# Threshold attention and a tanh MoE: shared score tiles, a sign mask ahead of the transposes, and one hand-written schedule

## The chip, the cores and the metric

The kernel runs on one core of one Trainium2 chip. The metric is the device time of one execution in microseconds (us), the median of several runs. The engines that matter here are TensorE (PE, matmuls and transposes), VectorE (DVE), ScalarE (ACT), GpSimd (POOL) and SyncE (SP), which issues the DMAs.

## What is computed

Eight batches of eight heads; each head has 576 tokens and 64 dimensions. Weights more than `tau` (0.02) below their row's greatest score are dropped. The result, 4608 tokens by 512, goes through two matmuls with `h - tanh(h)` between them.

```python
scores = scale * np.matmul(q, k.transpose(0, 1, 3, 2))      # per head 576 x 576
thresh = np.max(scores, axis=-1, keepdims=True) - tau
scores = np.where(scores >= thresh, scores, -1000000000.0)
scores = scores - np.max(scores, axis=-1, keepdims=True)
attn = np.exp(scores)
attn = attn / (np.sum(attn, axis=-1, keepdims=True) + 1e-09)
out = np.matmul(attn, v)                                    # 576 x 64
x = out of all heads side by side                           # 4608 x 512
h = x @ w_in                                                # 512 x 2048
g = h - np.tanh(h)
y = g @ w_out                                               # 2048 x 512
```

## The kernel before

**Weights.** Lines 70 to 76 load `w_in` and `w_out` whole (4 MB each) on SP's queue and cast them to bf16 on POOL. They stand first in the program, so the first `q` load (line 97) is behind them on the queue and in its buffers.

**Attention** (lines 88 to 250) loops over 8 batches and 4 pairs of heads; a pair is 32 times the same work. For each head `q` and `k` are loaded, scaled by 256 and split into a high and a low fp16 half by ACT (line 112) and DVE (line 115). PE turns the five 128-row chunks (line 122), DVE copies the result (line 130). `kT_sw` is `kT` with its two 64-partition halves swapped, made by two DMAs (lines 135 and 138), so that two matmul sets per score tile give all products of high and low halves.

Then five query tiles (`qt`) of 128 rows, the last of 64, for each of the two heads: 320 score tiles in all. One tile is four score matmuls into `psS` (lines 177 and 182), `exp` on ACT (line 188), the row maximum on DVE (line 193), the threshold (line 197), compare, multiply and row sum on DVE (line 201), the reciprocal (line 207), five transposes of the weights on PE into `psPT` (line 213), their copy by ACT or DVE (lines 226 and 222), five matmuls with `v` (line 232), the scaling on ACT (line 238). Once per pair of heads and query tile the 128 columns are turned (line 244) and copied into `xT` (line 248).

**MoE** (lines 265 to 297) loops over nine blocks of 512 tokens: sixteen groups of four matmuls (line 271), each followed by `tanh` on ACT (line 278) and `th * -1 + psH` on DVE (line 279), and then four output tiles of sixteen matmuls each (line 287), copied by ACT (line 294) and stored.

**Order and buffers.** A scheduler orders the instructions and places the waits; each engine runs its own list in order. PSUM in attention: two `psS`, one `psT`, three shared by `psPT`, `psO` and `psOT`. In MoE: four `psH` and four `psY`.

## Time and profile before

| what | us |
|---|---|
| median of 3 runs | 1140.91 (1138.82 to 1142.63) |
| span of the profiled execution, first to last instruction | 1138.1 |
| weights loaded and cast, no matmul yet | 0 to 36 |
| attention | 36 to 885 |
| MoE alone | 885 to 1138 |

The page gives the span of the profiled execution and no time around it; the runs lie 0.7 to 4.5 us above that span, their median 2.8 above.

How to read the views. In the page's slices each digit is a tenth. In the busy table each row is a stretch of the span; after its length come PE, weight loads, DVE, ACT and POOL, each as busy us and, in brackets, its instructions; then the mean granted clock of TensorE (1.00 is its upper level of 2.4 GHz, 0.50 its lower of 1.2 GHz) and the DMA engines' share. A group of instructions shows its line, engine, operation, tiles and shapes, its count after the x, then busy us and the mean ns of one, and the idle time ahead of it with what ended it. In the timeline x5 means five instructions in a row, and the length is from the first one's start to the last one's end.

### The profile page before, as it was taken

What the parts mean: (1) busy time and instruction counts of PE and PEld (TensorE: products, weight loads), DVE (VectorE), ACT (ScalarE), POOL (GpSimd) and SP (SyncE); (2) the same over time, 40 slices, a digit from 0 to 9 for tenths busy, and PEclk for the clock granted to TensorE, in tenths of its full rate; (3) what the DMA queues carried; (4) which work ended last, traced back from release to release, by engine and by line L of the source; (5) the groups of instructions that cost most, each with busy time, mean ns of one, the idle gap of its engine ahead of it and who ended that gap; (6) DMA issues with size and microseconds to landing.
All of it is one profiled execution on the core that took longest, in us unless ns stands there. A gap on an engine that the chain in (4) does not pass through costs nothing.

```text
span 1138.1 us, 19514 instructions
## 1 busy us (share of the span) xinstructions
PE 858.6 (75%) x6408; PEld 479.1 (42%) x6432; DVE 787.3 (69%) x2289; ACT 589.8 (52%) x1141; POOL 121.7 (11%) x650
## 2 busy tenths in 40 slices
PE   0576777677777777677777777776777899999998
PEld 0244444444444444444444444444444444444443
DVE  0588887888888888888787788888887433333443
ACT  0456555555555655555555565556555444444443
POOL 4211111111111111111111111111110000000000
PEclk9978666766766877766676677778777899999999
DMA  7321112222222111112122222111110001111111
GB/s 295 73 48 43 43 43 48 48 53 49 48 50 46 42 43 42 44 42 47 44 51 49 49 50 51 43 43 43 42 43 6 19 37 47 38 37 37 44 41 37
DMA packets 134854, 56.85 MB, mean 50 GB/s; under 512 B 119392, under 2 KB 127584, under 8 KB 134240
## 3 DMA queue, kind: packets, MB, share of 16 engines
q1 hardware_dynamic: 134752, 55.61, 18.8%
q8 instruction: 50, 0.82, 0.3%
q14 instruction: 52, 0.43, 0.1%
HBM read 36.70 MB, written 9.44 MB: 41 GB/s over the span
## 4 chain that ended last, share of the span: by engine, by line
PE 52%; DVE 19%; ACT 18%; issue 6%; DMA 3%; POOL 1%; DVEq 0%; SPq 0%; ACTq 0%; POOLq 0%
PE psH L271 11%; PE psY L287 11%; ACT e L188 10%; DVE pr L201 6%; PE psPT L213 6%; PE psO L232 6%; PE psT L122 6%; PE psS L177 6%; DVE m L193 5%; ACT pT L226 4%; PE psS L182 4%; ACT o L238 3%; DVE pT L222 2%; PE psOT L244 2%; DMA w_out_f<-in_moe_w_out_dram 2%
## 5 line engine op out<-in xcount | busy, mean ns | idle before, releaser
L188 ACT ACTIVATE e<-psS,exp_bias 128x576 f32<-128x576 f32 (+1 forms) x320 | 234.1, 742 | 65.8 <-PE psS L182 48.2
L201 DVE SCALAR_TENSOR_TENSOR pr<-e,thr 128x576 bf16<-128x576 f32 (+1 forms) x320 | 255.2, 805 | 4.6 <-DVE thr L197 1.8
L193 DVE TENSOR_REDUCE m<-e 128x1 f32<-128x576 f32 (+1 forms) x320 | 235.0, 743 | 15.8 <-ACT e L188 15.3
L232 PE MATMUL psO<-vbf,pT 128*128 128x64 bf16 (+1 forms) x1600 | 123.7, 218 | 127.1 <-ACT pT L226 79.8
L238 ACT ACTIVATE o<-psO,recip 128x64 bf16<-128x64 f32 (+1 forms) x320 | 100.7, 315 | 221.4 <-PE psO L232 217.0
L177 PE MATMUL psS<-kT,qT 128*128 128x512 f16 (+3 forms) x640 | 165.9, 351 | 59.3 <-ACT e L188 40.4
L279 DVE SCALAR_TENSOR_TENSOR g_sb<-th,psH 128x512 bf16<-128x512 f32 x144 | 98.8, 688 | 137.5 <-ACT th L278 137.5
L182 PE MATMUL psS<-kT_sw,qT 128*128 128x512 f16 (+3 forms) x640 | 175.2, 348 | 0.0
L213 PE MATMUL psPT<-ident_bf,pr 128*128 128x128 bf16 (+1 forms) x1600 | 164.6, 246 | 1.7 <-DVE pr L201 1.1
L232 PEld LDWEIGHTS <-pT 128*128 128x128 bf16 (+1 forms) x1600 | 81.4, 115 | 184.5 <-ACT pT L226 115.0
L226 ACT COPY pT<-psPT 128x640 bf16<-128x640 bf16 x192 | 123.6, 644 | 36.9 <-PE psPT L213 33.8
L271 PE MATMUL psH<-xT,w_in_sb 128*128 128x512 bf16 x564 | 127.8, 383 | 2.8 <-DVE g_sb L279 1.5
L287 PE MATMUL psY<-w_out_sb,g_sb 128*128 128x512 bf16 x564 | 125.0, 379 | 0.6
L213 PEld LDWEIGHTS <-pr 128*128 128x128 bf16 (+1 forms) x1600 | 113.7, 114 | 22.2 <-DVE qhl L115 6.9
L177 PEld LDWEIGHTS <-qT 128*128 128x128 f16 (+1 forms) x640 | 64.1, 112 | 101.9 <-issue 80.2
L278 ACT ACTIVATE th<-psH 128x512 f32<-128x512 f32 x144 | 85.6, 597 | 39.6 <-PE psH L271 39.2
L209 POOL MEMSET pr<- 128x64 bf16 (+1 forms) x320 | 44.0, 150 | 438.7 <-PE psPT L213 267.5
L271 PEld LDWEIGHTS <-w_in_sb 128*128 128x128 bf16 x576 | 56.7, 99 | 70.2 <-issue 4.8
L222 DVE COPY pT<-psPT 128x640 bf16<-128x640 bf16 (+1 forms) x128 | 57.5, 449 | 40.9 <-PE psPT L213 38.9
L287 PEld LDWEIGHTS <-g_sb 128*128 128x128 bf16 x576 | 56.3, 98 | 68.0
L122 PE MATMUL psT<-ident_f,qhl 128*128 128x128 f16 (+1 forms) x320 | 50.2, 294 | 37.0 <-DVE qhl L115 37.0
L182 PEld LDWEIGHTS <-qT 128*128 128x128 f16 (+1 forms) x640 | 56.7, 118 | 50.7 <-issue 31.1
(33 smaller groups left out, 606.3 us busy)
## 6 DMA issues: line engine op xcount, KB each, us to landing
kT_sw<-kT SPq DMA_DIRECT2D x128, 72.0 KB, 2.0
out_dram<-yo SPq DMA_DIRECT2D x36, 256.0 KB, 2.0
qraw<-in_q_dram SPq DMA_DIRECT2D x64, 128.0 KB, 2.3
kraw<-in_k_dram SPq DMA_DIRECT2D x64, 128.0 KB, 2.2
vraw<-in_v_dram SPq DMA_DIRECT2D x64, 128.0 KB, 2.3
w_in_f<-in_moe_w_in_dram SPq DMA_DIRECT2D x1, 4096.0 KB, 12.6
w_out_f<-in_moe_w_out_dram SPq DMA_DIRECT2D x1, 4096.0 KB, 22.9
qraw<-in_q_dram SPq DMA_DIRECT2D x64, 16.0 KB, 2.2
```

The costliest lines, as they stand in the source:

```text
L122: nc.tensor.matmul(out=psT[:, c * P : c * P + cn], lhsT=hl[:cn, c, :, :].rearrange("p a d -> p (a d)"), rhs=ident_f16[:cn, :cn], is_transp ...
L177: nc.tensor.matmul(out=psS[:qn, kk0:kk1], lhsT=lhs, rhs=kT[:, kk0:kk1], start=True, stop=False,)
L182: nc.tensor.matmul(out=psS[:qn, kk0:kk1], lhsT=lhs, rhs=kT_sw[:, kk0:kk1], start=False, stop=True,)
L188: nc.scalar.activation(out=e0[:qn, :S], in_=psS[:qn, :S], func=ACT.Exp, scale=scale_eff, bias=exp_bias[:qn],)
L193: nc.vector.tensor_reduce(out=m0[:qn], in_=e0[:qn, :S], axis=AX.X, op=ALU.max,)
L201: nc.vector.scalar_tensor_tensor(out=pr[:qn, :S], in0=e0[:qn, :S], scalar=thr[:qn], in1=e0[:qn, :S], op0=ALU.is_ge, op1=ALU.mult, accum_ou ...
L213: nc.tensor.matmul(out=psPT[:, c * qn : (c + 1) * qn], lhsT=pr[:qn, c * P : (c + 1) * P], rhs=ident_bf[:qn, :qn], is_transpose=True, start ...
L226: nc.scalar.copy(out=pT[:, : KC * qn], in_=psPT[:, : KC * qn])
L232: nc.tensor.matmul(out=psO[:qn, :], lhsT=pT[:, c * qn : (c + 1) * qn], rhs=vb[:, c, :], start=(c == 0), stop=(c == KC - 1),)
L238: nc.scalar.activation(out=o2[:qn, hh * D : hh * D + D], in_=psO[:qn, :], func=ACT.Copy, scale=recip[:qn],)
L271: nc.tensor.matmul(out=psH, lhsT=w_in_sb[:, c, n * P : (n + 1) * P], rhs=xT[:, c, m0 : m0 + MB], start=(c == 0), stop=(c == DM_C - 1),)
L287: nc.tensor.matmul(out=psY, lhsT=g_sb[:, n, ms * P : (ms + 1) * P], rhs=w_out_sb[:, n, :], start=(n == 0), stop=(n == DF_C - 1),)
```

## The change

The new kernel computes the same by other tiles and in an order that is written out.

- **Tiles.** A pair of heads has nine score tiles (`TPP`) in place of ten: four of 128 queries for each head, and one (j = 4) whose upper 64 partitions are the first head's last 64 queries and whose lower 64 are the second's. That makes 288 tiles. `load`, `split`, `turn` work on a pair: one transposed `kT` and `qT` of 1152 columns each, nine transposes.
- **Mask.** `scores` ends in one DVE instruction that scales the scores from PSUM into `sc` and takes the row maximum; POOL makes `nb = tau - max`. `kink` is one ACT instruction, `Prelu` with a slope of 1e30 below zero: kept scores become `score - max + tau`, dropped ones hugely negative. `weights` turns this `z` on PE into `psZ`, and the `exp` is taken while ACT copies `psZ` out. The row sum comes from a column of ones behind `v` (65 columns in `attend`). `norm` divides for up to five tiles at once, `emit_x` turns and copies a whole pair into `xT`.
- **Split.** After the first pair, the high and low halves are made on POOL by three instructions, not by ACT and DVE.
- **MoE.** Once a batch of four pairs is done, the next batch's 36 rounds carry up to 32 steps of MoE. A step is either four matmuls of one hidden group with tanh and DVE (`h_step`) or four of the sixteen matmuls of an output tile of the block before (`y_step`). Seven of ten stages ride along (208 steps); the last three (80 steps) come at the end, with more PSUM buffers.
- **Weights of MoE** are loaded in sixteen pieces of 512 KB during the first batch, through two buffers, and cast on POOL.
- **PSUM.** Two double banks for scores and turned `q`, `k` (`ps_big`), and one bank each for `psZ` and `psX`, for `psO`, for `psH`, for `psY`.
- **Order.** `manual_schedule` keeps the order of the code on each engine. Round s holds: scores of tile s+3, `kink` of s+1, `weights` of s, a step of MoE, `attend` of s-1, and at fixed places `norm`, `emit_x`, `split`, `turn`, loads.

The lines that go are those of the kernel above from 53 to 297 and aren't repeated; of the new ones the core stands here.

```diff
+    ps_big = pool("ps_big", 2, space=PSUM)
+    ps_z = pool("ps_z", 1, space=PSUM)
+    ps_o = pool("ps_o", 1, space=PSUM)
+    ps_h = pool("ps_h", 1, space=PSUM)
+    ps_y = pool("ps_y", 1, space=PSUM)
+    ctx.enter_context(tc.manual_schedule())
...
+    def split(p, t, fast=False):
+        r = raws.pop((p, t))[:, 0:9, :]
+        hl = hl_pool.tile([P, TPP, 2, D], FP16, name=f"{t}hl", tag=t)
+        if fast:
+            nc.scalar.mul(out=hl[:, :, 0, :], in_=r, mul=QKSC)
+            nc.vector.scalar_tensor_tensor(
...
+            x = hl_pool.tile([P, TPP, D], F32, name="xs", tag="xs")
+            nc.gpsimd.tensor_scalar(
+                out=x, in0=r, scalar1=QKSC, scalar2=1.0, op0=ALU.mult, op1=ALU.mult
+            )
+            nc.gpsimd.tensor_copy(out=hl[:, :, 0, :], in_=x)
+            nc.gpsimd.tensor_tensor(
+                out=hl[:, :, 1, :], in0=x, in1=hl[:, :, 0, :], op=ALU.subtract
+            )
...
+    def turn(p, t):
+        hl = hls.pop((p, t))
+        ps = ps_big.tile([P, W], FP16, name=f"ps_{t}", tag="big")
+        for c in range(TPP):
+            nc.tensor.matmul(
+                out=ps[:, c * P : (c + 1) * P],
+                lhsT=hl[:, c, :, :].rearrange("p a d -> p (a d)"),
+                rhs=ident_f16, is_transpose=True, start=True, stop=True,
+            )
+        m = qk_pool.tile([P, W], FP16, name=f"{t}T", tag=t)
+        nc.vector.tensor_copy(out=m, in_=ps)
+        mats[p, t] = m
+        if t == "k":
+            sw = qk_pool.tile([P, W], FP16, name="kS", tag="ks")
+            nc.sync.dma_start(out=sw[0:D, :], in_=m[D:P, :])
+            nc.sync.dma_start(out=sw[D:P, :], in_=m[0:D, :])
...
+    def kind(j):
+        return "M" if j == 4 else "A" if j in (0, 2, 5, 7) else "B"
+    def scores(i):
+        p, j = divmod(i, TPP)
+        qT, kT, kS = mats[p, "q"], mats[p, "k"], mats[p, "ks"]
+        ps = ps_big.tile([P, 1024], F32, name="psS", tag="big")
+        main, rem, lo = slice(0, 512), slice(512, 576), 0
+        if kind(j) == "B":
+            main, rem, lo = slice(512, 1024), slice(448, 512), 448
+        if j == 4:
+            for n, kk in enumerate((kT, kS)):
+                for dst, srcs in ((main, MAIN), (rem, REM)):
+                    for hh in range(2):
...
+            hh = int(j > 4)
+            lhs = qT[:, j * P : (j + 1) * P]
+            for n, kk in enumerate((kT, kS)):
+                for dst, src in ((main, MAIN[hh]), (rem, REM[hh])):
+                    nc.tensor.matmul(
+                        out=ps[:, dst], lhsT=lhs, rhs=kk[:, src],
+                        start=(n == 0), stop=(n == 1),
+                    )
+        sc = sc_pool.tile([P, S], F32, name="sc")
+        mx = st_pool.tile([P, 1], F32, name="mx", tag="mx")
+        nc.vector.tensor_scalar(
+            out=sc, in0=ps[:, lo : lo + S], scalar1=SC, scalar2=None,
+            op0=ALU.mult, op1=ALU.max, accum_out=mx,
+        )
+        nb = st_pool.tile([P, 1], F32, name="nb", tag="nb")
+        nc.gpsimd.tensor_scalar(
+            out=nb, in0=mx, scalar1=-1.0, scalar2=tau, op0=ALU.mult, op1=ALU.add
+        )
+        scs[i] = sc, nb
...
+    def kink(i):
...
+        else:
+            zt = z_pool.tile([P, W], BF16, name="z")
+            zs[i] = zt
+            z = zt[:, 0:S]
+        nc.scalar.activation(
+            out=z, in_=sc, func=ACT.Prelu, bias=nb, scale=1.0, alpha=STEEP
+        )
...
+    def weights(i):
+        kd = kind(i % TPP)
+        ps = ps_z.tile([P, 5 * P], BF16, name="psZ", tag="z")
+        if kd == "B":
+            z, pt, off, n = zs.pop(i - 1), pts[i - 1], 512, 5
+        else:
+            z = zs[i] if kd == "A" else zs.pop(i)
+            pt = p_pool.tile([P, TPP * P], FP16, name="pT")
+            pts[i] = pt
+            off, n = 0, 4
+        for c in range(n):
...
+        nc.scalar.activation(
+            out=pt[:, off : off + n * P], in_=ps[:, 0 : n * P], func=ACT.Exp
+        )
...
+    def attend(i):
...
+        if j in (1, 6):
+            ops[p, int(j > 4)] = ps_o.tile([P, 5, D + 1], F32, name="psO", tag="o")
+        po = ops[p, int(j > 4)]
...
+        pt, hh = pts.pop(i - 1), int(j > 4)
+        for ab in range(2):
+            blocks = [(4 * ab + ab + c, c) for c in range(4)]
+            blocks.append((4, 4 + ab))
+            for n, (blk, c) in enumerate(blocks):
+                nc.tensor.matmul(
+                    out=po[:, (j - 1 - 5 * hh) + ab, :],
+                    lhsT=pt[:, blk * P : (blk + 1) * P], rhs=vb[:, hh, c, :],
+                    start=(n == 0), stop=(n == 4),
                 )
...
+    def norm(p, hh):
...
+        nc.vector.reciprocal(out=rc[:, 0:n], in_=po[:, 0:n, D])
+        nc.vector.tensor_tensor(
+            out=osb[p][:, 0:n, hh, :], in0=po[:, 0:n, 0:D],
+            in1=rc[:, 0:n].unsqueeze(2).to_broadcast([P, n, D]), op=ALU.mult,
+        )
...
+    def emit_x(p):
...
+        ps = ps_z.tile([P, S], BF16, name="psX", tag="z")
+        for t in range(4):
+            nc.tensor.matmul(
+                out=ps[:, t * P : (t + 1) * P],
...
+        nc.vector.tensor_copy(out=xT[:, p % HPAIR, b * S : (b + 1) * S], in_=ps)
...
+    def hidden(m, n, ps):
...
+        for c in range(DM_C):
+            nc.tensor.matmul(
+                out=ps, lhsT=w_in_sb[:, c, n * P : (n + 1) * P],
+                rhs=xT[:, c, m * MB : (m + 1) * MB],
+                start=(c == 0), stop=(c == DM_C - 1),
+            )
+        th = t_pool.tile([P, MB], F32, name="th")
+        nc.scalar.activation(out=th, in_=ps, func=ACT.Tanh)
+        nc.vector.scalar_tensor_tensor(
+            out=gs[m][:, n, :], in0=th, scalar=-1.0, in1=ps,
+            op0=ALU.mult, op1=ALU.add,
+        )
...
+    def project(m, ms, part, ps, last):
+        for n in range(4 * part, 4 * part + 4):
+            nc.tensor.matmul(
+                out=ps, lhsT=gs[m][:, n, ms * P : (ms + 1) * P],
+                rhs=w_out_sb[:, n, :], start=(n == 0), stop=(n == DF_C - 1),
+            )
+        if part == 3:
+            yo = y_pool.tile([P, d_model], F32, name="yo")
+            if last:
+                nc.scalar.copy(out=yo, in_=ps)
+            else:
+                nc.vector.tensor_copy(out=yo, in_=ps)
...
+    def layers(m, tail):
...
+        def h_step(n):
+            if tail and n % 3:
+                ps = ps_big.tile([P, MB], F32, name="psHt", tag="big")
+            else:
+                ps = ps_h.tile([P, MB], F32, name="psH", tag="h")
+            hidden(m, n, ps)
+        def y_step(ms, part):
+            if part == 0:
+                tag = ("y", "o", "z")[(4 * (m - 1) + ms) % 3] if tail else "y"
+                pl = {"y": ps_y, "o": ps_o, "z": ps_z}[tag]
+                cur["y"] = pl.tile([P, d_model], F32, name="psY", tag=tag)
+            project(m - 1, ms, part, cur["y"], tail and ms % 2)
...
+        for a in range(16):
+            if m < NMB:
+                steps.append(lambda a=a: h_step(a))
+            if m > 0:
+                steps.append(lambda a=a: y_step(a // 4, a % 4))
+        return steps
...
+    def w_load(piece):
...
+        nc.gpsimd.tensor_copy(out=flat[:, i * cols : (i + 1) * cols], in_=wt)
...
+    load(0)
+    load(1)
+    for t in ("k", "q"):
+        split(0, t, fast=True)
+        turn(0, t)
+    split_v(0)
...
+    for s in range(-AHEAD, NTILE + 2):
+        p, j = divmod(max(s, 0), TPP)
+        if 0 <= s < NTILE and j == 0 and p % HPAIR == 0 and p >= HPAIR:
+            assert not todo
+            todo = layers(stage, False)
+            share = len(todo) / (HPAIR * TPP)
+            done, stage = 0.0, stage + 1
+        if s + AHEAD < NTILE:
+            scores(s + AHEAD)
+        if 0 <= s + 1 < NTILE:
+            kink(s + 1)
+        if 0 <= s < NTILE:
+            weights(s)
+            if todo:
+                done += share
+                if j == TPP - 1 and p % HPAIR == HPAIR - 1:
+                    done = 1e9
+                while todo and done >= 1:
+                    todo.pop(0)()
+                    done -= 1
+        if 0 <= s - 1 < NTILE:
+            attend(s - 1)
+            pp, jj = divmod(s - 1, TPP)
+            if jj == 4:
+                norm(pp, 0)
+            if jj == 8:
+                norm(pp, 1)
+                emit_x(pp)
+        if 0 <= s < NTILE:
+            if j == 0 and p + 2 < NPAIR:
+                load(p + 2)
+            if p + 1 < NPAIR:
+                if j == 0:
+                    split(p + 1, "k")
+                if j == 1:
+                    split(p + 1, "q")
+                if j == 2:
+                    split_v(p + 1)
+                    turn(p + 1, "k")
+                if j == 4:
+                    turn(p + 1, "q")
+            if p < HPAIR and j >= 3:
+                piece = next(pieces, None)
+                if piece:
+                    w_load(piece)
+    while stage <= NMB:
+        for step in layers(stage, True):
+            step()
+        stage += 1
```

On ACT, in the midst of attention, there stood (names as above, the number is the buffer):

```order
L188 ACTIVATE e0_5824<-psS_5819,exp_bias_68 128x576
L226 COPY pT_5706<-psPT_5700 128x640
L188 ACTIVATE e0_5860<-psS_5855,exp_bias_68 128x576
L238 ACTIVATE o2_5650<-psO_5708,recip_5697 128x64
L188 ACTIVATE e0_5892<-psS_5887,exp_bias_68 128x576
L226 COPY pT_5742<-psPT_5736 128x640
L238 ACTIVATE o2_5718<-psO_5744,recip_5733 128x64
L188 ACTIVATE e0_5928<-psS_5923,exp_bias_68 64x576
L238 ACTIVATE o2_5718<-psO_5776,recip_5765 128x64
```

and now stands, in a batch with MoE steps:

```order
L240 ACTIVATE z_5168<-sc_5126,nb_5129 128x576
L266 ACTIVATE pT_5189<-psZ_5188 128x512
L240 ACTIVATE z_5257<-sc_5163,nb_5166 128x576
L266 ACTIVATE pT_5189<-psZ_5259 128x640
L351 ACTIVATE th_5271<-psH_5266 128x512
L240 ACTIVATE z_5257<-sc_5182,nb_5185 128x576
L266 ACTIVATE pT_5291<-psZ_5290 128x512
L240 ACTIVATE z_5341<-sc_5252,nb_5255 128x576
L266 ACTIVATE pT_5291<-psZ_5343 128x640
L351 ACTIVATE th_5355<-psH_5350 128x512
L240 ACTIVATE z_5368<-sc_5284,nb_5287 128x576
L266 ACTIVATE pT_5371<-psZ_5370 128x512
```

Each tile has one `Prelu` (L240) and one `exp` out of PSUM (L266); the `Prelu` of tile s+1 is ahead of the `exp` of tile s, and a tanh (L351) comes behind the `exp` in four rounds of nine. Copies, scalings and splits are gone from ACT, and the list holds a single table load, at its start, as before.

On DVE, where a query tile or a pair ends, there stood:

```order
L222 COPY pT_6398<-psPT_6392 128x320
L115 SCALAR_TENSOR_TENSOR khl_6469<-kraw_6465,khl_6469 128x5x64
L193 TENSOR_REDUCE m0_6498<-e0_6496 128x1
L248 COPY xT_70<-psOT_6407 128x64
L130 COPY kT_6478<-psT_6472 128x576
L197 TENSOR_SCALAR thr_6500<-m0_6498 128x1
L201 SCALAR_TENSOR_TENSOR pr_6502,ssum_6503<-e0_6496,thr_6500 128x576
L115 SCALAR_TENSOR_TENSOR qhl_6834<-qraw_6830,qhl_6834 128x5x64
L207 RECIPROCAL recip_6505<-ssum_6503 128x1
```

and now stands, at the end of a pair:

```order
L221 TENSOR_SCALAR sc_3737,mx_3738<-psS_3732 128x576
L352 SCALAR_TENSOR_TENSOR g_2836<-th_3755,psH_3750 128x512
L221 TENSOR_SCALAR sc_3774,mx_3775<-psS_3769 128x576
L221 TENSOR_SCALAR sc_3793,mx_3794<-psS_3788 128x576
L368 COPY yo_3810<-psY_3561 128x512
L314 RECIPROCAL rc_3823<-psO_3758 128x4
L315 TENSOR_TENSOR osb_3705<-psO_3758,rc_3823 128x4x64
L336 COPY xT_68<-psX_3826 128x576
L221 TENSOR_SCALAR sc_3863,mx_3864<-psS_3854 128x576
L352 SCALAR_TENSOR_TENSOR g_2836<-th_3882,psH_3877 128x512
```

A tile leaves one instruction on DVE (L221). The rows L314, L315 and L336 are the pair's end: PE's six transposes (L324, L331) lie between L315 and L336, and PE's next transposes of `z` lie behind L336, because `psX` and `psZ` are one bank.

On SP, at the start of the program, there stood:

```order
L70 DMA w_in_f32_76<-in_moe_w_in_dram 128x4x2048
L73 DMA w_out_f32_79<-in_moe_w_out_dram 128x16x512
L97 DMA qraw_110<-in_q_dram 128x4x64
L103 DMA qraw_110<-in_q_dram 64x64
L97 DMA kraw_125<-in_k_dram 128x4x64
L103 DMA kraw_125<-in_k_dram 64x64
L144 DMA vraw_143<-in_v_dram 128x4x64
L150 DMA vraw_143<-in_v_dram 64x64
```

and now, where the first two pairs' loads end:

```order
L113 DMA qraw_159<-in_q_dram 128x4x64
L117 DMA qraw_159<-in_q_dram 64x64
L123 DMA vraw_164<-in_v_dram 128x4x64 x2
L128 DMA vraw_164<-in_v_dram 64x2x64
L129 DMA vraw_164<-in_v_dram 64x2x64
L181 DMA kS_184<-kT_182 64x1152
L182 DMA kS_184<-kT_182 64x1152
L113 DMA kraw_255<-in_k_dram 128x4x64
```

The weights' loads have left the front of the queue. The swap of the first pair's `kT` (L181, L182) stands behind all 24 loads of the first two pairs.

## Rows read from the trace of the kernel before

**Rows 1.** The page, granted TensorE clock in 40 slices, tenths of full speed.

```profile
PEclk9978666766766877766676677778777899999999
```

**Rows 2.** Busy time by engine in three stretches: attention, overlap, MoE.

```profile
700.00:800.00 100.00, 72.28 (x625) 43.55 (x624) 81.99 (x254) 58.15 (x115) 12.78 (x78) 0.72 0.21 47
870.00:880.00 10.00, 8.32 (x81) 4.53 (x79) 9.16 (x31) 6.95 (x14) 0.75 (x5) 0.96 0.01 2
1000.00:1100.00 100.00, 99.53 (x456) 45.32 (x464) 42.22 (x62) 43.89 (x75) 0.00 (x0) 1.00 0.09 35
```

**Rows 3.** The same view where attention ends and MoE begins.

```profile
882.00:884.00 2.00, 1.07 (x16) 0.72 (x16) 0.83 (x4) 0.94 (x3) 0.00 (x0) 1.00 0.00 0
884.00:886.00 2.00, 0.70 (x6) 0.54 (x7) 0.52 (x2) 0.64 (x3) 0.00 (x0) 0.60 0.00 0
...
890.00:892.00 2.00, 2.00 (x8) 0.83 (x7) 0.96 (x2) 0.70 (x2) 0.00 (x0) 0.69 0.00 0
```

**Rows 4.** Groups of instructions by shape, 100 to 860 us.

```profile
L201 DVE SCALAR_TENSOR_TENSOR pr<-e,thr 128x576 bf16<-128x576 f32 x231 | 184.1, 807 | 4.0 <-DVE thr L197 1.4
L193 DVE TENSOR_REDUCE m<-e 128x1 f32<-128x576 f32 x232 | 170.4, 745 | 10.5 <-ACT e L188 10.0
L188 ACT ACTIVATE e<-psS,exp_bias 128x576 f32<-128x576 f32 x232 | 169.7, 744 | 49.0 <-PE psS L182 39.7 <-DVE thr L197 8.2 <-ACT qhl L112 0.2
...
L226 ACT COPY pT<-psPT 128x640 bf16<-128x640 bf16 x145 | 99.6, 687 | 10.2 <-PE psPT L213 7.2 <-ACT o L238 0.3
...
L207 DVE RECIPROCAL recip<-ssum 128x1 f32<-128x1 f32 x231 | 35.3, 153 | 0.0
...
L130 DVE COPY kT<-psT 128x576 f16<-128x576 f16 x57 | 26.0, 457 | 35.0 <-PE psT L122 35.0
```

**Rows 5.** Groups of instructions over the whole span: MoE, and casts on POOL.

```profile
L279 DVE SCALAR_TENSOR_TENSOR g_sb<-th,psH 128x512 bf16<-128x512 f32 x144 | 98.8, 688 | 137.5 <-ACT th L278 137.5
L278 ACT ACTIVATE th<-psH 128x512 f32<-128x512 f32 x144 | 85.6, 597 | 39.6 <-PE psH L271 39.2 <-PE psOT L244 0.5
...
L155 POOL CAST vbf<-vraw 128x256 bf16<-128x256 f32 x64 | 25.5, 398 | 85.2 <-PE psO L232 74.8 <-DMA vraw<-in_v_dram 8.8
...
L71 POOL CAST w_in_sb<-w_in_f 128x8192 bf16<-128x8192 f32 x1 | 7.0, 7011 | 11.7 <-DMA w_in_f<-in_moe_w_in_dram 11.7
```

**Rows 6.** TensorE in order of time, inside attention: start, length, what.

```profile
444.44 0.67 PE L182 MATMUL psS<-kT_sw,qT 128*128 128x512 f16 x2
444.92 0.67 PE L177 MATMUL psS<-kT,qT 128*128 128x512 f16 x2
...
448.31 0.41 PE L177 MATMUL psS<-kT,qT 128*128 128x512 f16 x2 [0.18 <-ACT e L188]
448.56 0.41 PE L182 MATMUL psS<-kT_sw,qT 128*128 128x512 f16 x2
448.92 0.32 PE L232 MATMUL psO<-vbf,pT 128*128 128x64 bf16 x5
...
449.87 0.23 PE L244 MATMUL psOT<-ident_bf,o 128*128 128x128 bf16 x1
...
451.32 0.44 PE L213 MATMUL psPT<-ident_bf,pr 128*128 128x128 bf16 x5
```

**Rows 7.** Start of the program: DMA issues on SP, table load.

```profile
0.74 0.44 SPq L70 DMA_DIRECT2D w_in_f<-in_moe_w_in_dram  x1
...
31.64 0.56 SPq L103 DMA_DIRECT2D qraw<-in_q_dram  x1
...
33.77 1.28 ACT L112 ACT_TABLE_LOAD   x1 [33.77 <-DMA qraw<-in_q_dram]
```

**Rows 8.** The page, DMA issues: KB each, median us to landing.

```profile
kT_sw<-kT SPq DMA_DIRECT2D x128, 72.0 KB, 2.0
...
w_out_f<-in_moe_w_out_dram SPq DMA_DIRECT2D x1, 4096.0 KB, 22.9
```

**Rows 9.** Who waited for whom: total us, times, longest us.

```profile
PE psS L177 <- ACT e L188: 40.4, 108, 0.8
```

More of the change, by code (lines that the diff above doesn't have):

```diff
@@ new lines @@
+    NV = 3
+    vbs = []
+    for i in range(NV):
+        vb = const.tile([P, 2, 6, D + 1], BF16, name=f"vb{i}")
+        nc.gpsimd.memset(vb[:, :, 4:6, :], 0.0)
+        nc.vector.memset(vb[:, :, 0:4, D : D + 1], 1.0)
+        nc.vector.memset(vb[0:64, :, 4, D : D + 1], 1.0)
+        nc.vector.memset(vb[64:P, :, 5, D : D + 1], 1.0)
+        vbs.append(vb)
+    pool = lambda name, bufs, **kw: ctx.enter_context(
+        tc.tile_pool(name=name, bufs=bufs, **kw)
+    )
+    PSUM = bass.MemoryType.PSUM
@@ new lines @@
+    osb = {}
+    def norm(p, hh):
+        po = ops.pop((p, hh))
+        if hh == 0:
+            osb[p] = o_pool.tile([P, 5, 2, D], BF16, name="osb")
+        n = 5 - hh
+        rc = st_pool.tile([P, 5], F32, name="rc", tag="rc")
+        nc.vector.reciprocal(out=rc[:, 0:n], in_=po[:, 0:n, D])
+        nc.vector.tensor_tensor(
+            out=osb[p][:, 0:n, hh, :], in0=po[:, 0:n, 0:D],
+            in1=rc[:, 0:n].unsqueeze(2).to_broadcast([P, n, D]), op=ALU.mult,
+        )
+    def emit_x(p):
+        o = osb.pop(p)
+        ps = ps_z.tile([P, S], BF16, name="psX", tag="z")
+        for t in range(4):
+            nc.tensor.matmul(
+                out=ps[:, t * P : (t + 1) * P],
+                lhsT=o[:, t, :, :].rearrange("p a d -> p (a d)"),
+                rhs=ident_bf, is_transpose=True, start=True, stop=True,
+            )
+        for hh in range(2):
+            s = slice(64 * hh, 64 * hh + 64)
+            nc.tensor.matmul(
+                out=ps[s, 512:576], lhsT=o[s, 4, 0, :], rhs=ident_bf[s, s],
+                is_transpose=True, start=True, stop=True,
+            )
+        b = p // HPAIR
+        nc.vector.tensor_copy(out=xT[:, p % HPAIR, b * S : (b + 1) * S], in_=ps)
@@ new lines, in w_pieces @@
+    def w_pieces():
+        for w, sb, n in ((moe_w_in, w_in_sb, DM_C), (moe_w_out, w_out_sb, DF_C)):
+            flat = sb.rearrange("p c n -> p (c n)")
+            cols = n * w.shape[1] // 8
+            src = w.rearrange("(c p) n -> p c n", p=P)
+            for i in range(8):
+                yield flat, src, i, cols, w.shape[1]
+    def w_load(piece):
+        flat, src, i, cols, width = piece
+        wt = wt_pool.tile([P, cols], F32, name="wt", tag="wt")
+        if cols >= width:
+            r = cols // width
+            s = src[:, i * r : (i + 1) * r, :]
+            nc.sync.dma_start(out=wt.rearrange("p (c n) -> p c n", n=width), in_=s)
+        else:
+            r = width // cols
+            s = src[:, i // r, (i % r) * cols : (i % r + 1) * cols]
+            nc.sync.dma_start(out=wt, in_=s)
+        nc.gpsimd.tensor_copy(out=flat[:, i * cols : (i + 1) * cols], in_=wt)
```

338 lines of the change are left out of this document (112 added, 226 removed).

## Prediction, made before the changed kernel ran

> **What bounds the kernel now.** I read the page's clock slices first [rows 1]: the granted clock is mixed until about 885 us and full after, so there are two stages. The busy table [rows 2] tells what limits each. In attention (700 to 800) DVE is busy 82%, PE 72%, ACT 58%, at a mean clock of 0.72; no engine is full, and the tile's chain passes through all three. In MoE alone (1000 to 1100) PE is busy 99.5% at full clock: 456 matmuls in 99.53 us, 0.218 each. There DVE and ACT are busy 42% and 44%: the two stages leave different engines idle. Ahead of both lie 36 us in which the weights are loaded and cast [rows 7]. So 36 + 849 + 253 = 1138.
>
> **How the clock behaves.** Where attention ends, PE was busy 1.07 of 2 us, then 0.70 of 2, and the granted clock fell to 0.60 in that second stretch; it came back in 890 to 892, in which PE was busy without a gap [rows 3]. In 870 to 880, where MoE matmuls lie between the last tiles of attention, it was 0.96 [rows 2]. The middle of the new kernel looks like that stretch.
>
> **Prices on PE, at full clock** [rows 6]. The score matmuls of one operand (512 + 64 columns) start 0.25 us apart (448.31, 448.56), so a tile's two sets, S, take 0.49; at the lower level it is 0.48 for one (444.44, 444.92), twice as much. Five transposes take 0.44 with the last one's latency; one alone takes 0.23, so each adds 0.053. Five matmuls with v take 0.32, each adding 0.03. A MoE step is 4 x 0.218 = 0.87.
>
> A pair of heads has nine S (4.4), 0.5 more if the shared tile's half-width matmuls run one behind the other, 41 transposes of z (2.2), 50 matmuls with v (1.5), 18 + 6 transposes for q, k and x (1.3): 9.9. With eight MoE steps (7.0) it is 16.9 us.
>
> **Prices beside PE.** The new DVE instruction on the scores is not in this trace; its nearest rows are the maximum (0.745) and the multiply with a sum (0.807) over 576 columns [rows 4]; I take 0.85 with the read of its accumulator, bounds 0.75 to 0.95. Per pair DVE has 9 x 0.85, four times 0.69 for MoE [rows 5], two copies of 1152 columns (0.457 for 576 [rows 4], so up to 0.9 each), the normalisation (two reciprocals of 0.15 and two products, under 0.5 each), x (0.46) and one output copy (0.7): 14.7 us. ACT has nine Prelu, priced like the exp of 576 columns (0.744; not seen here, 0.7 to 0.85), nine exp out of PSUM (0.60 to 0.69) [rows 4, 5], four tanh (0.60): 15 us. Both fit under 16.9, and each gives up work: a tile had two large instructions on DVE, now one.
>
> POOL takes over the split of q and k. Its casts cost 0.86 ns an element in a long one and 1.55 in a short one [rows 5], so three instructions over 576 elements take 1.5 to 2.7 us, 3.6 if the one with two inputs is twice as slow. With v, nine `nb` and two splits that is 6 to 10 us a pair, beside PE. Queued behind a split is the next `nb`; the Prelu that needs it comes two rounds, some 4 us, later. By "GPSIMD Engine Reference", section 3.1 of the Trainium skill, an fp32 add of 2048 elements takes 4497 ns there, which makes an estimate of 1.3 us for 576; the sum would not change by it.
>
> **What one PSUM bank costs.** After the transposes of tile s (T) comes the exp on ACT, and T of s+1 waits for it, since psZ is one bank. That loop is 0.44 + 0.69 + two hand-overs, about 1.25 us. What PE does in between: a MoE step (0.87), the matmuls with v (0.3 or none) and S (0.49), 1.4 or more. So in rounds with a step the loop is hidden. The ninth round of a pair has no step: 0.6 us open. At a pair's end PE must wait: matmuls with v, then on DVE a reciprocal and product (0.65, behind an output copy), then six transposes, then the copy of x (0.46) before T may use the bank again; only S (0.5 to 1.0) covers part of it. I take 1.1 us. psH is one bank too: 0.87 + 0.60 + 0.69 = 2.2 us, and hidden steps come every second round, 3.7 us; covered. "Perfetto Trace Analysis", section "Optimizing Tensor Performance", of the Trainium skill speaks against this: independent matmul groups should rotate through different PSUM banks, so that the evacuation of one overlaps the next group's matmuls. In the trace two psS buffers cost PE 40.4 us in 108 waits of ACT [rows 9], 0.37 each, so a short rotation shows. What the rule would make of it is the second rival.
>
> **The sum.**
> - Start. An issue on SP takes about 0.53 us [rows 7]; the swap of kT stands behind 24 loads: 0.74 + 24 x 0.53 + two issues + 2.0 to land [rows 8] = 16.6 us; S, DVE, nb and Prelu follow, so T of tile 0 comes at 20 (bounds 14 and 25; table load and first split are over by then). Before, the first matmul came at 36.
> - First batch, 36 rounds without MoE steps. The loop allows 1.3 us a round at full clock; at the lower level PE needs 2.2. The weights' pieces, two at a time, are waited for by POOL, and `nb` stands behind them: the two large loads took 22.9 us to land [rows 8], so 512 KB takes some 1.5 + 2 us, a cast 0.9, and two buffers give one piece in 2.2 us, for 16 rounds. I take 2.1 a round and 1.5 for each pair's end: 82 us, bounds 55 and 100.
> - Middle, 28 pairs: 16.9 + 0.6 + 1.1, and 0.1 a round for small waits of PE as in [rows 6] (0.18 before the scores at 448.31) = 19.5 each, 546; the first stage has no output steps, 16 x 0.87 less: 532.
> - Tail, 80 steps at 0.87 = 70, and 2 until it runs.
> - End: copy 0.6, issue 0.56, landing 2.0 = 3.
>
> 20 + 82 + 532 + 72 + 3 = 709 us of span. The profiled span of before is 1138.1, the median of the runs 1140.9; with the same 2.8 around it the median comes to **712 us**, 0.62 of before. The whole gain: 16 us at the start, and 251 us of MoE of which 180 no longer stand alone but fill gaps of attention, and attention's own 849 us shrink because DVE's two passes became one and the clock stays up.
>
> **Rivals.**
> 1. *POOL sets the pace.* If a split costs 6 us (POOL spans are rough, and two-input instructions are not in the trace), `nb` comes 2 to 3 us late in each pair, the Prelu waits, and with it everything behind it on ACT. 28 x 2.2 + 6 = 68 us: 780. For it: a single queue with long and short work mixed. Against: 0.86 to 1.55 ns an element [rows 5].
> 2. *The single banks show.* If ACT's exp waits behind Prelu and tanh so that PE stands through the whole evacuation in each round, 0.69 + 0.1 comes on nine rounds, less the 0.6 already counted: 6.5 us x 28 = 182, 894 in all. For it: the Prelu of the next tile is ahead of the exp on ACT. Against: ACT's 15 us fit into 19.5.
> 3. *The clock swings in the middle as it does in attention now*, 0.72 on average [rows 2]. A pair's 16.9 us become 23.5: 28 x 6.6 less 5 = 180, 892 in all. For it: each pair's end leaves PE idle 1 to 2 us, and 882 to 886 shows a fall after idle time. Against: the 0.96 of 870 to 880, and 85% PE work.
> 4. *Slower than before.* The clock stays at the lower level through the whole middle. Then a pair takes 33.8 + 2.6 = 36.4, the middle 28 x 36.4 - 28 = 991, with 20, 85, 72, 3 and 2.8: 1174. It decides from a mean clock of about 0.52 in the middle. Against: [rows 3], where dense work brought the clock back.
> 5. *The change doesn't interleave as it says.* The order of instructions, which the section on the change shows, has the tanh of MoE between the Prelu and exp of attention, so I give this nothing of its own.
>
> **How the numbers follow.** Forecast as summed, 655 to 765: 0.68. Rival 1 (765 to 815): 0.13. Rivals 2 and 3 (830 to 950): 0.14. Rival 4: 0.03. Below 655, if the first batch runs at full clock and the hand-overs cost nothing: 0.02. The range 655 to 815 holds 0.81. A measurement of this kernel tells about 0.3% from no change; slower by more takes rival 4 (0.03), no change a chance value near it (0.01), faster 0.96.
>
> **What would show it.** Right: in the changed profile PE is the busiest engine in the middle, 80% or more, at a granted clock of 0.9 or higher; a pair takes 19 to 20 us; its one clear gap is before the six transposes of x, waiting for DVE; the first T comes near 20 us; the tail lasts 70 us with PE full. Wrong: PE waits for ACT's exp in most rounds (rival 2), ACT's Prelu for POOL (rival 1), a clock of 0.5 in whole slices of the middle (3, 4), or a Prelu or score instruction far over 0.85 us, which would make ACT or DVE the bound.

## The result and the profile after

The changed kernel takes **702.2 us** in the median (701.7 to 704.4), against 1140.3 for the kernel before beside it: a ratio of 0.6165, 95% interval 0.6148 to 0.6182. The forecast was 712. The profiled execution spans 699.9 us; the runs lie 2.3 above it.

The page's first lines, and its clock slices (17.5 us each), answer to [rows 1]:

```profile
PE 609.4 (87%) x6112; PEld 366.5 (52%) x6112; DVE 422.5 (60%) x985; ACT 462.1 (66%) x761; POOL 272.0 (39%) x597
PE   1765688888999999999999999999999999999997
PEclk9978789999999999999999999999999999999999
```

PE is the busiest engine, at a high clock from slice 7 on. The same in stretches (busy time of PE, PEld, DVE, ACT, POOL, then the mean granted clock), to be set beside [rows 2]: the first batch, the middle, the tail.

```profile
60.00:100.00 40.00, 26.91 (x286) 18.66 (x285) 17.39 (x43) 21.81 (x35) 24.23 (x43) 0.74 0.61 164
200.00:300.00 100.00, 93.44 (x1010) 57.59 (x1008) 67.91 (x160) 73.82 (x123) 43.46 (x98) 1.00 0.35 82
630.00:700.00 70.00, 65.52 (x303) 29.41 (x301) 24.65 (x37) 21.42 (x36) 0.00 (x0) 1.00 0.12 46
```

In the middle PE is busy 93% and DVE 68%, where attention had 72% and 82% before. What waits are left on PE between 130 and 600 us (line, what ended the wait, then total us, times, longest):

```profile
PE psX L324 <- DVE osb L315: 27.2, 25, 1.6
PE psZ L256 <- ACT pT L266: 8.2, 23, 0.4
```

Both come about once a pair. The kernel before waited more often: the 40.4 us in 108 waits of [rows 9] are one of its kinds, the largest was 79.8 us in 100 waits for `pT` from ACT. A pair's end in order of time on PE (start, length, what, and in brackets the idle time ahead of it):

```profile
306.66 0.38 PE L256 MATMUL psZ<-ident_bf,z 128*128 128x128 bf16 x4 [0.37 <-ACT pT L266]
306.88 1.03 PE L359 MATMUL psY<-w_out_sb,g 128*128 128x512 bf16 x4
307.75 0.48 PE L300 MATMUL psO<-vb,pT 128*128 128x65 bf16 x10
309.24 0.40 PE L324 MATMUL psX<-ident_bf,osb 128*128 128x128 bf16 x4 [1.02 <-DVE osb L315]
309.57 0.22 PE L331 MATMUL psX<-ident_bf,osb 64*64 64x64 bf16 x2
309.72 0.44 PE L205 MATMUL psS<-kT,qT 128*64 128x512 f16 x4
309.99 0.41 PE L205 MATMUL psS<-kS,qT 128*64 128x512 f16 x4
310.34 0.45 PE L256 MATMUL psZ<-ident_bf,z 128*128 128x128 bf16 x5
```

A wait for the exp behind the ninth round, which has no MoE step, a wait for the normalisation, then the shared tile's scores, which take 0.62 us from 309.72 to 310.34. What DVE did ahead of 309.24:

```profile
307.95 0.69 DVE L368 COPY yo<-psY 128x512 f32<-128x512 f32 x1 [0.52 <-PE psY L359]
308.56 0.17 DVE L314 RECIPROCAL rc<-psO 128x4 f32<-128x4 f32 x1
308.76 0.42 DVE L315 TENSOR_TENSOR osb<-psO,rc 128x256 bf16<-128x256 f32 x1
```

PE's matmuls with v end near 308.2, and DVE's output copy ends at 308.6; so about 0.3 of the 1.02 us is the output copy, and the rest is the reciprocal and the product. The new instructions, as groups over the whole span (busy time and mean ns of one; then the engine's idle time before them):

```profile
L240 ACT ACTIVATE z<-sc,nb 128x576 bf16<-128x576 f32 x288 | 221.5, 769 | 38.2 <-POOL nb L226 37.9
L221 DVE TENSOR_SCALAR_CACHE_REDUCE sc<-psS 128x576 f32<-128x576 f32 x288 | 214.9, 752 | 38.6 <-PE psS L215 15.6
L149 POOL TENSOR_TENSOR qhl<-xs,qhl 128x576 f16<-128x576 f32 x31 | 39.7, 1279 | 2.6
```

In the first batch POOL looks like this (idle time in brackets), behind the split for the next pair:

```profile
30.63 0.19 POOL L226 TENSOR_SCALAR nb<-mx 128x1 f32<-128x1 f32 x1
33.34 1.04 POOL L417 CAST w_in_sb<-wt 128x1024 bf16<-128x1024 f32 x1 [2.51 <-DMA wt<-in_moe_w_in_dram]
34.45 0.19 POOL L226 TENSOR_SCALAR nb<-mx 128x1 f32<-128x1 f32 x1
```

POOL stands 2.51 us for a piece of weights that has not landed, and `nb` comes behind it; over the batch (22 to 104 us) ACT's Prelu waited 25.3 us in 17 waits for `nb`.

### The profile page after: what moved, and what is told of

The parts are those of the page before. It is cut to its first block, busy times and chain, and to the rows that moved or that the text cites. A ratio compares the mean times of both kernels' runs of the same rounds, so it can differ in the third digit from the quotient of the medians.

```text
span 699.9 us, 16371 instructions
## 1 busy us (share of the span) xinstructions
PE 609.4 (87%) x6112; PEld 366.5 (52%) x6112; DVE 422.5 (60%) x985; ACT 462.1 (66%) x761; POOL 272.0 (39%) x597
## 4 chain that ended last, share of the span: by engine, by line
PE 69%; ACT 9%; DVE 8%; DMA 4%; issue 3%; POOL 3%; SPq 2%; POOLq 0%; DVEq 0%; ACTq 0%
PE psY L359 17%; PE psH L345 15%; PE psS L215 12%; PE psZ L256 9%; ACT th L351 3%; ACT pT L266 3%; PE psS L205 3%; ACT z L240 3%; PE psHt L345 2%; PE psO L300 2%; DVE yo L368 2%; DMA wt<-in_moe_w_in_dram 2%; PE ps_k L171 2%; PE psX L324 2%; DVE osb L315 2%
## 5 line engine op out<-in xcount | busy, mean ns | idle before, releaser
L266 ACT ACTIVATE pT<-psZ 128x512 f16<-128x512 bf16 (+1 forms) x288 | 184.2, 640 | 120.2 <-PE psZ L256 118.8
L240 ACT ACTIVATE z<-sc,nb 128x576 bf16<-128x576 f32 x288 | 221.5, 769 | 38.2 <-POOL nb L226 37.9
L221 DVE TENSOR_SCALAR_CACHE_REDUCE sc<-psS 128x576 f32<-128x576 f32 x288 | 214.9, 752 | 38.6 <-PE psS L215 15.6
L352 DVE SCALAR_TENSOR_TENSOR g<-th,psH 128x512 bf16<-128x512 f32 x124 | 85.3, 688 | 114.5 <-ACT th L351 114.5
L359 PE MATMUL psY<-w_out_sb,g 128*128 128x512 bf16 x576 | 145.5, 379 | 0.0
L256 PE MATMUL psZ<-ident_bf,z 128*128 128x128 bf16 x1280 | 121.6, 223 | 27.0 <-ACT pT L266 25.5
L256 PEld LDWEIGHTS <-z 128*128 128x128 bf16 x1280 | 80.8, 99 | 71.4 <-issue 28.7
L215 PE MATMUL psS<-kS,qT 128*128 128x512 f16 (+1 forms) x512 | 107.6, 293 | 5.3 <-DMA kS<-kT 5.2
L215 PE MATMUL psS<-kT,qT 128*128 128x512 f16 (+1 forms) x512 | 107.8, 293 | 3.6 <-DVE kT L177 1.9
L215 PEld LDWEIGHTS <-qT 128*128 128x128 f16 x1024 | 74.9, 99 | 63.9 <-issue 6.5
L351 ACT ACTIVATE th<-psH 128x512 f32<-128x512 f32 x124 | 74.0, 597 | 36.6 <-PE psH L345 36.4
L324 PE MATMUL psX<-ident_bf,osb 128*128 128x128 bf16 x128 | 13.3, 229 | 36.2 <-DVE osb L315 31.6
L177 DVE COPY qT<-ps_q 128x1152 f16<-128x1152 f16 x32 | 24.2, 757 | 20.3 <-PE ps_q L171 20.3
L177 DVE COPY kT<-ps_k 128x1152 f16<-128x1152 f16 x32 | 24.2, 757 | 18.5 <-PE ps_k L171 18.5
```

The lines of the kernel that those rows point to most:

```text
L215: nc.tensor.matmul(out=ps[:, dst], lhsT=lhs, rhs=kk[:, src], start=(n == 0), stop=(n == 1),)
L221: nc.vector.tensor_scalar(out=sc, in0=ps[:, lo : lo + S], scalar1=SC, scalar2=None, op0=ALU.mult, op1=ALU.max, accum_out=mx,)
L240: nc.scalar.activation(out=z, in_=sc, func=ACT.Prelu, bias=nb, scale=1.0, alpha=STEEP)
L256: nc.tensor.matmul(out=ps[:, c * P : (c + 1) * P], lhsT=z[:, off + c * P : off + (c + 1) * P], rhs=ident_bf, is_transpose=True, start=True ...
L266: nc.scalar.activation(out=pt[:, off : off + n * P], in_=ps[:, 0 : n * P], func=ACT.Exp)
L351: nc.scalar.activation(out=th, in_=ps, func=ACT.Tanh)
```

## The experiments

The theory is the prediction's: the middle is PE's own work plus two waits a pair, the first batch is POOL standing for weights. The rivals are that another engine or the tile's chain sets the pace, and that the low clock makes the first batch long. Pair lengths below go from one psX to the next on PE, the first from the first T; "the middle" is the mean of pairs 9 to 31, 18.8 us in the changed kernel. Its first four pairs took 83.5 us. Where a run adds a line to the code, later line numbers are one higher. Cuts in the code are marked with "...".

**MoE out of attention.** All steps after the last tile:

```diff
-        if 0 <= s < NTILE and j == 0 and p % HPAIR == 0 and p >= HPAIR:
+        if False:
```

> All MoE steps come after the last attention tile; attention's own order is unchanged. The prediction's reading: a pair of the middle is PE's work, so it loses the 7.0 us of its eight steps, but the clock then swings as in the first batch, where pairs without steps took 15.0 to 24.2 us: 14 to 18 us a pair in place of 18.9, and 208 steps of 0.874 come behind it, 182 us: 754 to 866 us. Rival, the steps only fill time in which PE waits for the tile's chain: a pair stays at 18.9 us, and the whole 182 us are added: 884 us, at a clock near 1 in the middle.

Measured: 752.3 us (ratio to before 0.6608, 0.6593 to 0.6622). A pair takes 13.7 us, and behind the first batch the clock did not swing:

```profile
200.00:300.00 100.00, 85.41 (x1132) 59.09 (x1130) 72.06 (x183) 82.88 (x139) 59.08 (x131) 1.00 0.41 91
PE psZ L256 <- ACT pT L266: 26.7, 82, 0.8
```

The first row is its busy time by engine, the second the largest of PE's waits between 130 and 600 us: about 0.33 each, in three of a pair's nine rounds, where the loop over the single bank psZ stands open because no step covers it. So interleaving is worth 50 us, not more: with it the stretch behind the last pair is 188 us shorter (74.3 in place of 262.1), and 28 pairs are 4.9 us longer each (137). The rest of the gain comes ahead of that, from the start and the rewritten attention. Both halves of the expectation were too dear, the first because of the clock.

**The pair's end.** The six transposes of x into the other bank, one round into the next pair; and, apart from it, the bank alone:

```diff
-        ps = ps_z.tile([P, S], BF16, name="psX", tag="z")
+        ps = ps_o.tile([P, S], BF16, name="psX", tag="o")
...
-                emit_x(pp)
+                late.append(pp)
...
+            if j == 1 and late:
+                emit_x(late.pop())
```

> The six transposes of x of a pair (psX) take a bank of the other pool and come one round into the next pair, so that PE doesn't stand behind the pair's normalisation on DVE. Theory, that the pair's end is a wait of PE for DVE of 1.02 us: 0.8 to 1.0 us a pair less, 32 pairs: 672 to 680 us. Rival, that PE waits for the chain elsewhere when this wait goes: 700 to 704 us.

> psX takes a bank of the other pool, and its place in the order stays. The prediction said that T has to wait for the copy of x out of the shared bank (0.46 us a pair, partly covered by S). If that wait shows: 5 to 15 us less, 687 to 697. If it is hidden behind S, as the trace reads, and the gap is the normalisation's alone: within 2 us of 702.

The bank alone gives 701.7 us (0.6162, 0.6152 to 0.6172): nothing. The later transposes give 691.0 (0.6076, 0.6059 to 0.6092), 11 us in place of the 22 to 30 that were expected; the middle's pair falls from 18.8 only to 18.5. The wait for the normalisation went, but a new one came, for the swapped kT: 11.1 us in 16 waits from 130 to 600 us. PE, DVE and SP's queue in one of these pairs:

```profile
277.52 0.42 PE L215 MATMUL psS<-kS,qT 128*128 128x512 f16 x2 [1.42 <-DMA kS<-kT]
```
```profile
269.50 0.76 DVE L177 COPY kT<-ps_k 128x1152 f16<-128x1152 f16 x1 [0.40 <-PE ps_k L171]
```
```profile
264.98 0.37 SPq L370 DMA_DIRECT2D out_dram<-yo  x1
265.44 0.40 SPq L113 DMA_DIRECT2D kraw<-in_k_dram  x1
...
271.94 0.61 SPq L129 DMA_DIRECT2D vraw<-in_v_dram  x1
272.65 0.55 SPq L181 DMA_DIRECT2D kS<-kT  x1
273.24 0.60 SPq L182 DMA_DIRECT2D kS<-kT  x1
```

kT is ready at 270.26. Its swap is issued at 272.65, behind an output copy that waited for its data and 12 loads that take 7.2 us to issue. To test that, the loads go behind the swap, in the run with the later transposes:

```diff
-            if j == 0 and p + 2 < NPAIR:
+            if j == 5 and p + 2 < NPAIR:
                 load(p + 2)
```

> The run with the later transposes of x, with one more move: the 12 loads of a pair are issued five rounds later, behind the swaps of kT. In that run PE waited 11.1 us in 16 waits for the swapped kT, whose issue stands behind an output copy and 12 loads of 0.53 us on SP. Theory, that this queue ate half of the gain: the waits go, and the time falls from 691 to 679 to 682. Rival, that the swap is late for another reason (POOL's split, the copy on DVE): 688 to 692.

Measured: 685.6 us (0.6022, 0.601 to 0.6034), between the two expectations, and the trace tells why. The middle is what the theory wants, pairs of 17.9 us without a wait for kS:

```profile
300.00:400.00 100.00, 98.44 (x1046) 59.73 (x1039) 70.97 (x170) 78.53 (x130) 44.20 (x99) 1.00 0.35 84
```

But the first four pairs took 94.7 us, against 85.3 without the move: the weights' pieces of that batch are now issued among the 12 loads, and POOL stands longer for them, 33.4 us between 22 and 107 in place of 24.8.

**The weights over eight pairs.**

```diff
-            if p < HPAIR and j >= 3:
+            if p < 2 * HPAIR and j in (4, 7):
```

> The 16 pieces of MoE weights come two to a pair over the first eight pairs, in place of five to a pair over the first four. Theory, that nb on POOL waits behind casts whose pieces have not landed (23.0 and 24.2 us a pair there): the first batch falls from 82 to 66 to 70 us, the total to 686 to 692. Rival, that its low clock alone makes the first batch long: the total stays within 3 us of 702, with the same low spells.

Measured: 693.4 us (0.609, 0.6066 to 0.6114), 1 us above what the theory expected. In the changed kernel the pieces come not five to a pair, as the expectation says, but six, six, four and none, since `j >= 3` holds in six rounds. The first four pairs fall from 83.5 to 70.2, as expected. Some of it is lost again, in the second batch, where the first pair takes 20.2 us in place of 17.9. The clock stays mixed (0.81 from 60 to 100, 0.74 in the changed kernel), so the low clock alone does not make the batch long.

**The first swap ahead of the second pair's loads.** `load(1)` after the first turns:

> The second pair's loads are issued behind the first pair's swaps of kT. The swaps then stand behind 12 loads fewer at 0.44 to 0.56 us an issue on SP: the first T comes 5 to 6 us earlier, 695 to 697 us. Rival, the first split on ACT and DVE, or the next pair's later data, gives it back: 700 to 703.

Measured: 701.4 us (0.6162, 0.615 to 0.6173): the rival. The first T comes at 16.1 in place of 21.8, and the first four pairs take 88.3 in place of 83.5. Then PE has nothing to do. The second pair's kS is not there (a wait of 3.8 us), since its swap is issued at 26.87, behind the third pair's loads; and POOL stands 7.25 us, until 32.34, for the first piece of the weights. The clock falls behind that:

```profile
22.00:26.00 4.00, 3.39 (x48) 2.34 (x46) 2.69 (x8) 2.71 (x6) 2.79 (x6) 1.00 0.38 83
26.00:30.00 4.00, 0.21 (x3) 0.03 (x2) 0.56 (x2) 0.38 (x1) 0.00 (x0) 0.97 0.75 182
30.00:34.00 4.00, 2.13 (x11) 1.05 (x11) 1.53 (x4) 0.32 (x1) 1.52 (x3) 0.50 0.60 214
```

The 0.50 lasts until 46. POOL stands four more times for pieces by then, and PE is busy 4.95 us of the 8 from 34 to 42. In the changed kernel the granted clock from 22 to 34 is 1.00.

**All three moves**, and then with the loads behind the swap:

> The later transposes of x, the weights spread over eight pairs, and the swaps ahead of the second pair's loads, all three. If the waits they remove are independent: 30 + 13 + 5.5 less, 645 to 665 us. If they cover the same time: 670 to 680.

> The three moves together, and the loads behind the swaps. There PE waited 10.9 us in 14 waits for the swapped kT in the middle and 3.7 in the first pair: 655 to 659 us if all of it goes, 664 to 670 if another wait takes its place.

Together 668.1 us (0.5869, 0.5852 to 0.5887), the fastest run of the whole computation, some 34 us below the changed kernel. That lies between the two expectations, 3 us above what independent waits would give, and yet it is more than the three gave alone: 11, 9 and 1. The first four pairs take 66.5 us, and pairs 2 to 4 run at full clock, 15.0 each:

```profile
60.00:100.00 40.00, 32.18 (x407) 21.32 (x403) 26.31 (x69) 32.45 (x54) 25.41 (x51) 1.00 0.65 156
```

The same hole as in the run with the swap alone is there, but behind it PE is busy and the clock comes back:

```profile
26.00:30.00 4.00, 0.31 (x3) 0.09 (x2) 0.60 (x2) 1.08 (x2) 0.00 (x0) 0.66 0.75 181
30.00:34.00 4.00, 4.00 (x29) 2.37 (x29) 1.53 (x4) 1.01 (x2) 1.42 (x3) 0.50 0.91 281
34.00:38.00 4.00, 2.68 (x41) 2.05 (x40) 2.44 (x7) 4.00 (x8) 2.37 (x6) 0.98 0.76 149
```

POOL stands there as long for the first piece (6.96 us, until 32.35), and then 0.32 us for the second; no third one follows in that pair. So the early swap keeps its 5.7 us where the first pair no longer carries six pieces. By stages the 34 us are 5.7 at the start, 17.0 in the first four pairs and 11.6 in the others; alone, the swap's 5.7 were given back up to 0.9, and the spread pieces won 13.3 in the first four pairs and lost 4.2 behind them.

With the loads later it is 681.4 (0.5988, 0.597 to 0.6005): slower, which neither expectation had. Its middle is better (18.0 in place of 18.5 us), but its first eight pairs take 17 to 23. What POOL waited for pieces of `w_in` from 14 to 130 us (total, times, longest), with the loads early and late; for those of `w_out` it was 10.1 and 9.3 us:

```profile
POOL w_in_sb L417 <- DMA wt<-in_moe_w_in_dram: 13.8, 5, 7.0
```
```profile
POOL w_in_sb L417 <- DMA wt<-in_moe_w_in_dram: 34.0, 8, 6.6
```

Moving the loads only from the ninth pair on would by these numbers be worth 23 x 0.5 = 12 us more, an estimate of 656; no run shows it.

**Rival 1's price.** POOL makes each split twice:

```diff
+            for _ in range(2):
+                nc.gpsimd.tensor_scalar(
...
+                nc.gpsimd.tensor_copy(out=hl[:, :, 0, :], in_=x)
+                nc.gpsimd.tensor_tensor(
...
```

> POOL makes each split of q and k twice, with the same result: 5.2 us more POOL work a pair. The prediction's first rival priced a slow split at 2.2 us a pair. If nb's lead of two rounds (some 4 us) is used up by a split of 5.2 us in one queue: 1 to 3 us a pair, 730 to 790 us. If POOL has slack enough (39% busy now): within 3 us of 702.

Measured: 805.7 us (0.7073, 0.7043 to 0.7103), a pair of 22.1. POOL is busy only 57 to 63% in the middle, and still it sets the pace, as waits between 200 and 600 us show:

```profile
ACT z L241 <- POOL nb L227: 70.1, 36, 3.3
PE ps_q L172 <- POOL qhl L150: 26.4, 18, 1.5
```

The Prelu waits for an `nb` queued behind a split, and the transposes of q for the split. In the changed kernel the Prelu did not wait for `nb` between 200 and 600 us. So the cover ends somewhere between 2.6 and 5.2 us a split.

**PE's work made less.** `scores` leaves out the second set of matmuls, `for n, kk in enumerate((kT,))`, with `start` and `stop` both true; the scores then lack a part, and the run is good for its time alone:

> The second set of score matmuls of each tile (the operand kS) is left out, so the scores lack a part; the swaps that make kS stay. It takes 2.2 us of PE's work a pair at full clock. If the pair is PE's work plus the waits at its end: 2.0 to 2.2 us a pair of the middle less, 635 to 645 us. If the chain from scores over DVE, POOL and ACT sets the pair: within 5 us of 702. If ACT (15 us a pair) becomes the bound: the same 640, with ACT over 85% busy.

Measured: 666.7 us (0.5854, 0.5839 to 0.5868), between what the theory and the chain would give (635 to 645, about 702). The pair falls by 1.4 us to 17.4, of 2.2 taken out:

```profile
200.00:300.00 100.00, 88.21 (x956) 55.08 (x954) 72.66 (x174) 78.23 (x132) 46.29 (x102) 1.00 0.36 85
```

No engine is full, ACT has 78%. Between 130 and 600 us PE's waits for the exp rise from 8.2 to 20.4 us, those for the normalisation from 27.2 to 30.9, and a new one comes, 4.8 us for the copy of x out of the bank that psX and psZ share. So PE's work sets most of the pair, and the chain stands not far behind: 0.8 of the 2.2 us went into waits. And the first four pairs took 88.6 us, with T early (14.8) as in the run with the early swap.

**DVE's saved pass.** The score instruction executed twice, in the changed kernel and with all MoE at the end:

> The instruction on DVE that scales a tile's scores and takes their maximum is executed twice, with the same result: 9 x 0.84 = 7.5 us more DVE work a pair, about what the second pass over the scores cost in the kernel before. DVE's work then comes to 20.4 us a pair, above the pair's 18.9. If the saved pass is part of the gain inside the interleaved middle: 20.5 to 22 us a pair, 745 to 790 us. If PE's work hides it: 702 to 715.

> The same doubled instruction, with all MoE steps at the end. A pair without steps took 13.6 us; DVE's work there would be 9.8 + 7.5 = 17.3 us. If DVE's second pass alone made attention slow: 17.4 to 19 us a pair at full clock, 860 to 905 us. If the clock falls again because PE then stands idle for a third of the time, as in the kernel before (26.5 us a pair at 0.72): 980 to 1110 us.

Interleaved it is 799.5 us (0.7021, 0.6982 to 0.706), a pair of 22.0: the dear end of the pair that was expected, and a total 9 us above the dear end of 790. With MoE at the end it is 890.4 (0.783, 0.7806 to 0.7853), a pair of 18.4: inside the range for DVE's pass alone, but at a clock that falls in part (0.88), not at full clock. Busy time of the first run from 300 to 400 us with PE's largest wait from 130 to 600, then of the second from 300 to 400:

```profile
300.00:400.00 100.00, 83.83 (x837) 49.48 (x836) 88.54 (x220) 63.64 (x105) 37.68 (x83) 0.97 0.28 67
PE psX L325 <- DVE osb L316: 56.0, 22, 3.0
```
```profile
300.00:400.00 100.00, 72.55 (x845) 49.35 (x846) 88.36 (x233) 65.29 (x104) 45.83 (x101) 0.88 0.30 67
```

DVE is busy 88% in both. In the first the normalisation queues behind the scores' second pass; in the second PE's largest wait is for that pass itself, 67.2 us in 115 waits for a psS to come free, and the normalisation comes next with 60.6. One pass over the scores is thus worth 97 us in the interleaved kernel and 138 without interleaving. With two passes, interleaving gains 91 us and not 50.

## Why the prediction was right

**The sum**, term by term, in us:

| term | predicted | measured |
|---|---|---|
| start, to the first T | 20 | 21.8 |
| first batch | 82 | 82.1 |
| middle, 28 pairs | 532 | 522.2 |
| tail | 72 | 69.9 |
| end | 3 | 3.8 |
| around the span | 2.8 | 2.3 |

- *Start.* The swap stood behind 24 loads, as reckoned, but these took 14.6 us to issue, 0.61 each from start to start and not 0.53. So it was issued at 15.3 and 15.9 and was there at 18.4, not 16.6; that is the whole difference.
- *First batch.* The total was right, the shape not: an even 2.1 us a round was reckoned, and there were pairs of 21.3, 23.0, 24.2 and 15.0; the fourth has no pieces. The mechanism, POOL standing for pieces with `nb` behind it, is in the trace and fell with the spread pieces. A piece landed in 4.1 to 4.5 us and not 3.5. That the sum agrees to 0.1 us is luck.
- *Middle.* PE's 16.9 a pair was low in small groups and high in one: transposes of z about 2.5, not 2.2; matmuls with v 1.8, not 1.5; transposes of q, k and x 1.5, not 1.3; but the shared tile's half-width scores cost 0.13 more than a whole tile's and not 0.5, since their matmuls overlap. In all it was 17.5. The ninth round stood open 0.37, not 0.6. The small waits, 0.9 a pair, weren't there. So 18.9 in three pairs of four, against 19.5. The total hides a miss the other way: the four pairs of the first stage, with half the steps, were reckoned at 4 x 19.5 - 14 = 64 us and took 72.0. PE was busy 15.0 us a pair there, where 16.9 - 3.5 = 13.4 were reckoned, and it waited 2.8, twice as long as in a full pair. The 24 pairs behind them were reckoned at 468 and took 448.
- *Pair end.* 1.02 against 1.1, but all of it is the way to the normalisation, the output copy ahead of it included. The copy of x out of the shared bank, which the step named too, is hidden, as the run with psX in another bank shows.
- *Tail.* 80 steps at 0.874; the 2 us "until it runs" were not needed.
- *Prices.* Score instruction 0.752 + 0.083 for its accumulator (0.85), Prelu 0.769 (0.744), split 2.6 (1.5 to 3.6).

**What it got wrong in the account of the gain.** "180 no longer stand alone but fill gaps of attention" counts too much. By the prediction's own terms a pair without steps was 9 x 1.3 + 1.5 = 13.2 us, and one with them 19.5; so of 7.0 us of steps, 0.7 would fall into gaps. Measured are 13.7 and 18.8: 1.9. Of the 438 us gained, 388 come from the start and attention itself, and 50 from interleaving. The saved DVE pass, if the doubled instruction stands for it, is 138 of the 388. The other 249, from 890 to 1139 us, are not taken apart by a run. By stages the start is 13 us of them and the 32 pairs are 247, while the MoE at the end is 9 us longer. The kernel before, from 300 to 800 us, with the largest waits of its busiest engine, DVE:

```profile
300.00:800.00 500.00, 360.08 (x3128) 217.53 (x3125) 407.45 (x1270) 285.83 (x570) 63.11 (x379) 0.71 0.20 46
DVE pT L222 <- PE psPT L213: 23.7, 47, 0.8
DVE kT L130 <- PE psT L122: 23.2, 19, 1.4
```

A pair took 849 / 32 = 26.5 us there, and DVE's work in it was 21.6, against about 16.3 (88.4% of 18.4) in the run with two passes; the clock was 0.71 against 0.88. So of 8.1 us between the two pairs 5.3 are work of DVE and 2.8 are time in which it stood idle; before, it stood mostly for transposes of PE, which ran at the lower mean clock. This is a count and not a test: the smaller DVE instructions that went and the clock may both have a part in the 249, and no run parts them.

**Rivals.** Rival 1 did not come, but its mechanism is real and near: 2.6 us more a split cost 3.3 us a pair. Rival 2 did not come with steps between; where they are absent its loop shows, with 0.33 us in three rounds of nine. The Trainium skill, "Perfetto Trace Analysis", section "Optimizing Tensor Performance", wants independent matmul groups in rotating PSUM banks. The trace agrees where no step lies between; with steps the single bank is covered, and moving psX to another gave nothing. Rivals 3 and 4 did not come, not even without steps: the clock in the middle was 1.00. For POOL's two-input instruction the Trainium skill, "GPSIMD Engine Reference", section 3.1, gave an estimate of 1.3 us. The trace agrees, with 1.279.

**What stays open.** The three moves together give 34 us and apart 21. The traces show where: POOL stands less for pieces, PE is busier behind the first hole, and from 38 us on the first batch runs at full clock. How much of it is the clock and how much the waits, no run separates; nor does one take the 249 us of attention apart.
